# A rank-15 channel product over 512 tokens at once, with token-row products on GpSimd, in an RWKV-6 and MLP-mixer kernel

## The chip, the core and the metric

The kernel runs on one core of a Trainium2 chip. The metric is the time of one execution in device microseconds; a comparison uses the median of several runs. The engines are TensorE (PE in the profile, its weight loads PEld), VectorE (DVE), ScalarE (ACT), GpSimd (POOL) and SyncE (SP). Each works off its own queue in order.

## The reference

```python
B, H, S, D = 4, 8, 768, 48        # batches, heads, tokens, head size; H * D = 384
for t in range(S):                # RWKV-6: a state of D x D per batch and head
    y[:, :, t] = r_t @ (state + (u * k_t) v_t^T)
    state = w_t[:, :, :, None] * state + k_t v_t^T
x = y, laid as (B, S, 384)
u = x + (relu(x^T @ w_tok1) @ w_tok2)^T           # token mixing, 768 -> 256 -> 768
out = u + relu(u @ w_ch1) @ w_ch2                 # channel mixing, 384 -> 1536 -> 384
```

All in float32.

## The kernel before

**Units.** The recurrence is cut into 12 units of 256 tokens, three to a batch. A unit runs two scans on VectorE over the decays w (`ends` with the reciprocal, L368 to L373, and `begins`, L380), multiplies keys and queries by their results (`keys` L377, `queries` L383), turns the keys on TensorE (`tokens`, L287, tile k_ps), forms outer products (`carry`, L303), carries the state (`updates` on VectorE, `scaled` on ScalarE, L438), and forms gram matrices (L257) and the outputs y_ps (`before` L317, `after` L338). `products` (L400, L402, L405) are three VectorE instructions per unit on the tile `near`: r times k, times u, summed over a head. In the last eight units they stand for the term of a token with itself; the tile is loaded by SP (`load_near`).

**Mixing.** Per batch: `hidden` and `back` are the token mixing (L522, L529), `turn` transposes its result into xT (L537). The first channel product is plain in the first batch (`up`, 256 tokens wide, L547). In the other batches it is `thirds`: 15 products (L585) of 4 matmuls each in place of a 3 by 3 by 2 block product's 18, for 256 tokens in two blocks of 128. `rights` makes the sums of its right sides on VectorE (L572, L499). Each product goes to a PSUM bank named x, y, z, u, v, w or q, several of which collect more than one; from there ScalarE copies (`take`, L590) or VectorE adds or subtracts (`plus` L593, `minus` L596, `rest` L599) into z, and ScalarE applies the relu (`done`, L602). A bank is written again only when the tap before has read it.

The second channel product is plain (`down`, 24 matmuls 384 wide, L624) for the first two of the first batch's three stretches of 256 tokens, and `quarters` otherwise: seven products p1 to p7 of six matmuls 192 wide (L642, L646) in place of a 2 by 2 block product's eight, with four sums of z on VectorE (L689, L690), three of them into tiles of their own, and with u2 and u3 summed on VectorE.

**Order.** It is written by hand: each batch is a list of pieces, and `woven` merges lists so that each is spread evenly by its pieces' costs; the merged order is the order of every engine's queue. The mixing of one batch is woven with the units of the next. In the first batch the sums of the weights (`weight_sums` L486, `left_sums` L503 to L508) are woven into the second channel product. PSUM has six banks for all of this (`ps_m`) and two for `carry`.

The order of the second and third batch is written in

```python
pieces = woven(hiddens + turned[:6] + sums[:3] + ..., a0 + a1 + a2 + b0)
for s, (att, near) in enumerate(((b1, n + 1), (b2 + c0, n + 2), (c1 + c2, n + 3))):
    ...
    pieces += ups[:1] + woven(ups[1:11], products_of(near) + sums[:2]) + ups[11:] + woven(att, ...quarters(s)...)
```

where a, b and c are the next batch's three units, each in three parts (0: loads and `ends`; 1: `keys` to `carry`; 2: `gram` to the end).

Of the kernel before, what the change touches and what calls it, by code (L numbers as in the profile page):

```python
# [62 lines left out]
def rwkv6_then_mixer(  # L63
# [48 lines left out]

    rks = [const.tile([128, 2 * COLS], f32, name=f"rk{i}") for i in range(3)]
# [37 lines left out]
    def load_near(i):  # L151
        if UB < i < NU:
            nears[i] = apool.tile([128, UC, 2, DM], f32, name="near", bufs=1)
            sp.dma_start(nears[i], near[i - UB - 1])
# [34 lines left out]
    early = [t.bitcast(u32) for t in halves]  # L189
    bits64 = [t[:, :4 * PIECE] for t in (scratch, spare, early[0])]  # L190
# [155 lines left out]
    def unit(i):  # L346
# [50 lines left out]
        def products(n):  # L397
            t = nears[i]
            if n == 0:
                dve.tensor_mul(t[:, :, 0], t[:, :, 0], t[:, :, 1])  # L400
            elif n == 1:
                dve.tensor_mul(t[:, :, 0], t[:, :, 0], u_rows.unsqueeze(1).to_broadcast([128, UC, DM]))  # L402
            else:
                L["sums"] = apool.tile([128, UC, H], f32, name="sums")
                dve.tensor_reduce(out=L["sums"], in_=nears.pop(i)[:, :, 0].rearrange("p c (h e) -> p c h e", e=D),  # L405
                                  axis=mybir.AxisListType.X, op=ALU.add)
# [58 lines left out]
        def each(f, n):  # L465
# [4 lines left out]
                    own_put=own_put, products=[lambda n=n: products(n) for n in range(3)], sums_put=sums_put,  # L470
# [4 lines left out]
    z_sums = [halves[0][:, ts(i, HJ * 128)].rearrange("p (j t) -> p j t", j=HJ) for i in range(3)]  # L475
    w_sums = [scratch[:, ts(i, HJ * HM)].bitcast(f32).rearrange("p (j e) -> p j e", j=HJ) for i in range(3)]
    parts = halves[0][:, ds(3 * HJ * 128, 3 * HM)].rearrange("p (n e) -> p n e", n=3)
    late_sums = [t.rearrange("p q x t -> p (q x t)")[:, :HJ * 128].rearrange("p (j t) -> p j t", j=HJ) for t in ats]
    late_sums.append(starts[:, :HJ * 128].rearrange("p (j t) -> p j t", j=HJ))
    late_parts = ws[0][:, :3 * HM].rearrange("p (n e) -> p n e", n=3)  # L480
# [32 lines left out]
    def mixing(bt, x_of, out_rows):  # L513
# [5 lines left out]
        def hidden(i, c):  # L519
            if c == 0:  # L520
                sums[i] = ps_m.tile([128, DM], f32, name="h1_ps", tag="m")
            pe.matmul(sums[i], wtok1[:, c, ts(i, 128)], x_of()[:, c, :], start=(c == 0), stop=(c == C - 1))  # L522
            if c == C - 1:
                act.activation(h1[:, i, :], sums.pop(i), AF.Relu)  # L524
# [15 lines left out]
        def up(s, jt, blocks=range(DM // 128)):  # L540
            if jt == 0 and 0 in blocks:
                zs[s] = halves[int((bt, s) != (0, 0))].rearrange("p (j t) -> p j t", j=NJ)
# [9 lines left out]
        def rights(s):  # L552
            b = lambda k, m: xT[:, k, ds(s * SEG + m * 128, 128)]
            if not last:
                four = h1.rearrange("p i e -> p (i e)")[:, :512] if s % 2 else rights_at[:, 8 * 128:]
                eight = rights_at[:, :8 * 128]
            elif s % 2 == 0:
                near = apool.tile([128, 12 * 128], f32, name="near", bufs=1)
                four, eight = near[:, :512], near[:, 512:]
            else:  # L560
                eight, four = apool.tile([128, 8 * 128], f32, name="to_end"), apool.tile([128, 4 * 128], f32, name="kT", bufs=1)
            h, f, e, g = (four[:, ts(n, 128)] for n in range(4))
            r12, r13, r9, r0, r4, r7, r2, r10 = (eight[:, ts(n, 128)] for n in range(8))
            of = {0: r0, 1: b(0, 1), 2: r2, 3: b(0, 0), 4: r4, 5: f, 6: b(2, 1), 7: r7, 8: b(1, 0), 9: r9, 10: r10, 11: e,
                  12: r12, 13: r13, 14: g}
            hfe = four[:, :3 * 128].rearrange("p (k t) -> p k t", k=3)
            first, second = (xT[:, :, ds(s * SEG + m * 128, 128)] for m in range(2))
            sums = ((dve.tensor_add, g, b(0, 1), b(1, 1)), (dve.tensor_add, hfe, first, second), (dve.tensor_sub, r12, b(0, 0), e),
                    (dve.tensor_sub, r13, b(0, 0), b(2, 0)), (dve.tensor_add, r9, r13, g), (dve.tensor_sub, r0, b(2, 1), b(1, 0)),
                    (dve.tensor_add, r4, f, h), (dve.tensor_sub, r7, h, e), (less, r2, b(1, 1), b(2, 1)),  # L570
                    (dve.tensor_add, r10, b(1, 0), b(2, 0)))
            return of, [(0.05, lambda q=q: q[0](*q[1:])) for q in sums]  # L572

        def thirds(s, of):
            z = halves[s % 2 if last else 1].rearrange("p (j t) -> p j t", j=NJ)
            to = lambda n: z[:, ts(n // 2, JB), ts(n % 2, 128)]
            banks = {}

            def product(r, name, end):
                first = name not in banks  # L580
                if first:
                    banks[name] = bank("z_ps").rearrange("p (q t) -> p q t", q=JB)
                ps = banks[name]
                for q in range(JB):
                    pe.matmul(ps[:, q], lefts[r][:, ts(q, 128)], of[r], start=first and q == 0, stop=end and q == JB - 1,  # L585
                              skip_group_check=True)
                return ps

            def take(n, ps):
                act.copy(to(n), ps)  # L590

            def plus(n, ps):
                dve.tensor_add(to(n), to(n), ps)  # L593

            def minus(n, ps):
                dve.tensor_sub(to(n), to(n), ps)  # L596

            def rest(n, ps):
                dve.tensor_sub(to(n), ps, to(n))  # L599

            def done(n, ps):
                act.activation(to(n), to(n), AF.Relu)  # L602

            order = ((14, "x", False, [(take, 3)]), (8, "y", False, [(take, 2)]), (12, "z", False, [(take, 4)]),
                     (9, "x", False, [(plus, 2)]), (0, "y", False, [(minus, 4)]), (4, "u", False, [(take, 0)]),
                     (13, "x", True, [(minus, 0), (take, 1)]), (5, "y", False, [(take, 5)]), (6, "v", False, [(plus, 5)]),
                     (7, "z", True, [(plus, 1)]), (2, "y", True, [(plus, 3), (done, 3)]), (10, "u", True, [(rest, 2), (done, 2)]),
                     (3, "w", True, [(minus, 0), (minus, 4), (done, 0)]), (1, "q", True, [(plus, 5), (plus, 1), (done, 5), (done, 1)]),
                     (11, "v", True, [(minus, 4), (done, 4)]))

            def one(r, name, end, taps):
                ps = product(r, name, end)
                for f, n in taps:
                    f(n, ps)

            return [(0.9, lambda q=q: one(*q)) for q in order]

        def down(s, n, jts):

            if jts[0] == 0:  # L620
                sums[n] = ps_m.tile([128, DM], f32, name="h2_ps", tag="m")
# [9 lines left out]
        def quarters(s):  # L631
            z = halves[s % 2 if last else 1].rearrange("p (j t) -> p j t", j=NJ)
            a11, a12, a21, a22 = (z[:, ts(j, HJ), ts(i, 128)] for i in range(2) for j in range(2))
            s1, s2, s4 = late_sums if last else z_sums
            t1, t2, t4 = w_sums
            m1, u2, u3 = ((late_parts if last else parts)[:, i] for i in range(3))
            L = {}

            def begin(a, b):
                L["q"] = ps_m.tile([128, HM], f32, name="q_ps", tag="m")  # L640
                for j in range(HJ // 2):
                    pe.matmul(L["q"], a[:, j, :], b[:, j, :], start=(j == 0), stop=False)  # L642

            def product(a, b):
                for j in range(HJ // 2, HJ):
                    pe.matmul(L["q"], a[:, j, :], b[:, j, :], start=False, stop=(j == HJ - 1))  # L646
                return L.pop("q")
# [4 lines left out]
            def p1():  # L652
                o = L["o"] = mpool.tile([128, 2, DM], f32, name="o", bufs=1)
                x = L["x"] = x_of()[:, ts(s, 2), :]
                act.copy(m1, product(a11, w11))
                dve.tensor_add(o[:, 0, :HM], x[:, 0, :HM], m1)

            def p4():
                o, x = L["o"], L["x"]
                dve.tensor_add(o[:, 1, :HM], x[:, 1, :HM], product(a22, t4))  # L660

            def p2():
                o = L["o"]
                dve.tensor_add(o[:, 0, :HM], o[:, 0, :HM], product(a12, w21))

            def p5():
                o, x = L["o"], L["x"]
                dve.tensor_add(o[:, :, HM:], x[:, :, HM:], product(s1, t1).unsqueeze(1).to_broadcast([128, 2, HM]))

            def p6():  # L670
                o = L["o"]
                dve.tensor_add(u2, m1, product(s2, t2))
                dve.tensor_add(o[:, 0, HM:], o[:, 0, HM:], u2)

            def p7():
                o = L["o"]
                both = o[:, 1].rearrange("p (n e) -> p n e", n=2)
                dve.tensor_add(u3, u2, product(a21, w12))
# [283 lines left out]
```

## Time and profile before

| | us |
|---|---|
| median of 3 runs (lowest, highest) | 517.13 (515.79, 517.88) |
| the profiled execution | 515.98 |
| its span | 514.3 |
| PE busy in the span | 489.3 (95%) |
| DVE busy | 388.3 (76%) |
| ACT busy | 229.3 (45%) |
| POOL busy | 1.3 |

The profile is of one execution; its span is from the first to the last instruction on the core, and the execution's own time is 1.7 us longer. A row of a group or of the timeline names the line of the kernel, the engine, the operation, the tile written and the tiles read. Each float32 matmul of the program has two rows. "Idle before" is the time in which an engine had nothing to run just before a row, with the instruction that ended it.

### The profile page before, as it was taken

The page shows a single profiled execution, that of the slowest core. Times are in us where ns is not written, and L with a number is a line of the kernel's source. Part 1 is how long each engine was busy: PE and PEld are TensorE (multiplying, and loading weights), DVE is VectorE, ACT ScalarE, POOL GpSimd, SP SyncE. Part 2 cuts the span into 40 slices and gives each one's busy share as a digit, 9 for nine tenths or more (in the row PEclk, how much of TensorE's full clock was granted, in tenths as well). Part 3 has the DMA queues.
Part 4 walks back from the last instruction along what each step waited for, and adds up shares of the span by engine and source line. Part 5 has one row for each costly group of instructions (what it writes and reads, how often), then busy time and mean ns, then how long its engine had stood idle before and what let it go on. Part 6 is the DMA issues. An engine that isn't in the chain of part 4 may idle for free.

```text
span 514.3 us, 13327 instructions
## 1 busy us (share of the span) xinstructions
PE 489.3 (95%) x5794; PEld 427.6 (83%) x5794; DVE 388.3 (76%) x633; ACT 229.3 (45%) x533; POOL 1.3 (0%) x10
## 2 busy tenths in 40 slices
PE   3489999999999999999999999999999999999996
PEld 2476688766789768999999868999999859999996
DVE  7999979959886878967888768977758616684653
ACT  3977685635353535434335445434335413531300
POOL 0000000000000000000000000000000000000000
PEclk9789999999999999999999999999999999999998
DMA  7945965352532342122212422100000000000000
GB/s 294 322 178 159 270 209 175 116 178 62 163 108 91 97 135 64 62 73 78 78 44 79 138 74 64 63 32 1 2 32 1 28 5 1 1 2 34 1 33 34
DMA packets 20945, 46.06 MB, mean 90 GB/s; under 512 B 2128, under 2 KB 13008, under 8 KB 20880
## 3 DMA queue, kind: packets, MB, share of 16 engines
q1 hardware_dynamic: 20736, 45.14, 27.4%
q8 instruction: 47, 0.77, 0.6%
q14 instruction: 18, 0.15, 0.1%
q10 hardware_dynamic: 144, 0.00, 0.0%
HBM read 40.41 MB, written 4.72 MB: 88 GB/s over the span
## 4 chain that ended last, share of the span: by engine, by line
PE 81%; DVE 12%; ACT 3%; issue 2%; DMA 1%; SPq 0%; DVEq 0%; ACTq 0%
PE z_ps L585 18%; PE q_ps L646 12%; PE q_ps L642 11%; PE z_ps L547 9%; PE h_ps L624 6%; PE h_ps L529 6%; PE h_ps L522 6%; PE gram L257 2%; PE y_ps L317 2%; PE y_ps L338 2%; PE kv_ps L303 2%; PE xT_ps L537 2%; DVE z L593 2%; DVE w L380 2%; ACT z L602 1%
## 5 line engine op out<-in xcount | busy, mean ns | idle before, releaser
L438 ACT ACTIVATE before<-state,to_end 112x48 f32<-112x48 f32 x176 | 44.5, 324 | 66.4 <-DVE state L448 61.0
L590 ACT COPY z<-z_ps 128x512 f32<-128x512 f32 x54 | 30.5, 586 | 57.5 <-PE z_ps L585 39.5
L593 DVE TENSOR_TENSOR z<-z,z_ps 128x512 f32<-128x512 f32 x54 | 35.9, 683 | 24.5 <-PE z_ps L585 15.9
L602 ACT ACTIVATE z<-z 128x512 f32<-128x512 f32 x54 | 33.3, 631 | 33.1 <-DVE z L593 29.0
L547 PE MATMUL z_ps<-xT,wch 128*128 128x256 f32 x216 | 48.1, 381 | 0.0
L547 PEld LDWEIGHTS z_ps<-xT,wch 128*128 128x128 f32 x216 | 40.5, 190 | 5.7
L646 PE MATMUL q_ps<-wch,z 128*128 128x192 f32 x222 | 43.3, 331 | 0.0
L642 PE MATMUL q_ps<-wch,z 128*128 128x192 f32 x222 | 42.8, 329 | 0.2
L642 PEld LDWEIGHTS q_ps<-wch,z 128*128 128x128 f32 x222 | 36.5, 190 | 0.9 <-ACT z L602 0.6
L646 PEld LDWEIGHTS q_ps<-wch,z 128*128 128x128 f32 x222 | 36.5, 190 | 0.6
L529 PE MATMUL h_ps<-h,wtok 128*128 128x384 f32 x96 | 34.9, 492 | 0.6 <-ACT h L524 0.6
L596 DVE TENSOR_TENSOR z<-z,z_ps 128x512 f32<-128x512 f32 x45 | 30.0, 683 | 7.0 <-PE z_ps L585 6.5
L522 PE MATMUL h_ps<-x,wtok 128*128 128x384 f32 x96 | 33.1, 492 | 0.0
L624 PE MATMUL h_ps<-wch,z 128*128 128x384 f32 x96 | 33.1, 493 | 0.0
L531 DVE TENSOR_TENSOR x<-x,h_ps 128x384 f32<-128x384 f32 x24 | 13.2, 551 | 24.5 <-PE h_ps L529 24.5
L585 PE MATMUL z_ps<-rk,wch 128*128 128x128 f32 x256 | 31.2, 275 | 0.0
L585 PEld LDWEIGHTS z_ps<-rk,wch 128*128 128x128 f32 x256 | 30.0, 192 | 0.0
L372 DVE TENSOR_TENSOR_SCAN to_end<-w,starts 112x1041 f32<-112x1041 f32 (+1 forms) x13 | 28.1, 2160 | 2.1 <-DMA w<-in_w_dram 1.7
L380 DVE TENSOR_TENSOR_SCAN w<-w,starts 112x1041 f32<-112x1041 f32 x12 | 27.8, 2321 | 0.0
L646 PE MATMUL q_ps<-scratch,z 128*128 128x192 f32 x144 | 27.8, 329 | 0.0
L642 PE MATMUL q_ps<-scratch,z 128*128 128x192 f32 x144 | 27.4, 327 | 0.0
L585 PE MATMUL z_ps<-xT,wch 128*128 128x128 f32 x216 | 27.1, 275 | 0.0
(183 smaller groups left out, 903.1 us busy)
## 6 DMA issues: line engine op xcount, KB each, us to landing
rk<-in_rk_dram SPq DMA_DIRECT2D x36, 192.0 KB, 3.9
near<-in_near_dram SPq DMA_DIRECT2D x8, 768.0 KB, 4.3
w<-in_w_dram SPq DMA_DIRECT2D x11, 520.5 KB, 3.8
vt<-in_v_dram SPq DMA_DIRECT2D x12, 384.0 KB, 3.4
out_dram<-o SPq DMA_DIRECT2D x24, 192.0 KB, 1.9
spare<-in_w_ch_dram SPq DMA_DIRECT2D x8, 512.0 KB, 4.8
scratch<-in_w_ch_dram SPq DMA_DIRECT2D x8, 512.0 KB, 4.8
rk<-in_rk_dram SPq DMA_DIRECT2D x6, 512.0 KB, 8.7
```

The source lines that it names most:

```text
L380: dve.tensor_tensor_scan(w_[:ROWS], w_[:ROWS], starts[:ROWS], 0.0, op0=ALU.mult, op1=ALU.add)
L438: act.mul(t[:ROWS, a], state[bt, g][:ROWS, a], by_last(c, j)[:, a:a + 1])
L522: pe.matmul(sums[i], wtok1[:, c, ts(i, 128)], x_of()[:, c, :], start=(c == 0), stop=(c == C - 1))
L529: pe.matmul(ps, wtok2[:, i, ts(c, 128)], h1[:, i, :], start=(i == 0), stop=(i == DTOK // 128 - 1))
L547: pe.matmul(ps, wch1[:, m, ts(jt, 128)], xT[:, m, ts(s, SEG)], start=(m == 0), stop=(m == DM // 128 - 1))
L585: pe.matmul(ps[:, q], lefts[r][:, ts(q, 128)], of[r], start=first and q == 0, stop=end and q == JB - 1, skip_group_check=True)
L590: act.copy(to(n), ps)
L593: dve.tensor_add(to(n), to(n), ps)
L602: act.activation(to(n), to(n), AF.Relu)
L624: pe.matmul(ps, zs[s][:, jt, ts(n, 128)], wch2[:, jt, :], start=(jt == 0), stop=(jt == NJ - 1))
L642: pe.matmul(L["q"], a[:, j, :], b[:, j, :], start=(j == 0), stop=False)
L646: pe.matmul(L["q"], a[:, j, :], b[:, j, :], start=False, stop=(j == HJ - 1))
```

## The change

The rank-15 product covers the first 512 tokens of a batch at once, in blocks of 256: `rights(0)` makes sums 256 wide, and `thirds(0)` goes through its left side in two halves (`at` 0 and 2), so that a bank still holds 128 x 512. The last 256 tokens keep blocks of 128. Some sums are made in place in xT.

`quarters` makes its sums in place in z; p1, p6 and p7 go one after the other into one PSUM bank (`chain`), from a pool of one (`ps_h`), and `ps_m` has five banks. The pool of one also takes bank z of `thirds`, one bank of `hidden` and one of `down`. The first batch's second stretch of 256 tokens gets `quarters` too, so that the sums of the weights move: sums 0 to 2 into the plain product, sum 3 and all ten left sums into the quarters after it.

In the second and third batch the two multiplications of `products` go to GpSimd, with the tile's load issued by ScalarE just before them; the sum over a head stays on VectorE, some ten products of the rank-15 product later. `ends` and `keys` of the second unit move from the front into the middle of the rank-15 product; the third unit's `ends` goes into the product of the last 256 tokens.

```diff
-        def products(n):
+        def products(n, by=dve):
...
-            b = lambda k, m: xT[:, k, ds(s * SEG + m * 128, 128)]
+            width = SEG if s == 0 else SEG // 2
+            b = lambda k, m: xT[:, k, ds(s * SEG + m * width, width)]
...
+            by_half = s == 0
+            count = JB // 2 if by_half else JB
...
-                for q in range(JB):
-                    pe.matmul(ps[:, q], lefts[r][:, ts(q, 128)], of[r], ...)
+                for q in range(count):
+                    pe.matmul(ps[:, q], lefts[r][:, ts(at + q, 128)], of[r], ...)
...
+            chain = (p1, p6, p7)
+
+            def begin(p, a, b):
+                if p in chain[1:]:
+                    L[p] = L[chain[0]]
+                else:
+                    L[p] = (held if p in chain else bank)("q_ps")[:, :HM]
+                half(0, L[p], a, b, first=p not in chain[1:])
...
+            of = {p1: (a11, w11), p4: (a22, t4), p2: (a12, w21), p5: (a22, t1), p6: (a11, t2), p7: (a21, w12), p3: (a12, w22)}
+            sum1 = (0.01, lambda: dve.tensor_add(a22, a21, a22))
+            two = [*ps[p1], *ps[p4], sum1] if start == 1 else [*ps[p4], sum1, *ps[p1]]
+            return [*two, (0.01, lambda: dve.tensor_sub(a21, a11, a21)),
+                    (0.01, lambda: dve.tensor_sub(a11, a22, a11)), *ps[p2], (0.01, lambda: dve.tensor_sub(a12, a12, a11)), *ps[p5], *ps[p6],
+                    *ps[p3], *ps[p7]]
...
-        downs = [plain(s) if bt == 0 and s < 2 else quarters(s) for s in range(S // SEG)]
+        downs = [plain(s) if (bt, s) == (0, 0) else quarters(s, 4 if (bt, s) == (0, 2) else 1) for s in range(S // SEG)]
...
     def products_of(i):
-        return [(1.0, f) for f in units[i]["products"]] + [(0.1, lambda: load_near(i + 1))] if i < NU else []
+        first, second, sums = units[i]["products"]
+        return [(0.1, lambda: load_near(i, act)), (0.1, lambda: first(by=pool)), (0.1, lambda: second(by=pool)), (1.0, sums)]
...
+        begin, scan, key, *b1 = *b0, *b1
+        loads, *c0 = c0
+        pieces = woven([e for h in hiddens for e in h] + turned[:5] + sums[:1] + turned[5:9], a0 + a1 + a2)
+        pieces += [begin, *sums[1:3], turned[9], *sums[3:]]
+        ups, first, second, third = with_turned(turned, thirds(0, of)), products_of(n + 1), products_of(n + 2), products_of(n + 3)
+        pieces += ups[:1] + first[:3] + ups[1:14] + first[3:] + ups[14:18] + [scan, key] + ups[18:20] + second[:3] + ups[20:31] + second[3:] + ups[31:]
+        of, sums = rights(2)
+        pieces += woven(b1, woven(quarters(0), sums))
+        ups = thirds(2, of)
+        pieces += ups[:1] + third[:3] + c0 + ups[1:14] + third[3:] + ups[14:]
+        pieces += woven(b2 + [loads] + c1 + c2, quarters(1) + quarters(2, 4))
...
-            mixed = downs[0][4:] + downs[1][:4] + woven(downs[1][4:] + ups[2], of_weights + [(0.1, f) for f in left_sums()])
+            left = [(0.1, f) for f in left_sums()]
+            mixed = woven(downs[0][4:], of_weights[:3]) + woven(downs[1], left[:3] + of_weights[3:] + left[3:]) + ups[2]
```

`with_turned` puts the last two `turn`s of a batch behind the first and second of the rank-15 product's pieces, and in the last batch the same `thirds(0)`, `quarters(0)`, `thirds(2)`, `quarters(1)`, `quarters(2, 4)` follow one another without units.

## The prediction

> **What bounds the kernel now.** I read the page first: busy times and the slices.
>
> ```profile
> PE 489.3 (95%) x5794; PEld 427.6 (83%) x5794; DVE 388.3 (76%) x633; ACT 229.3 (45%) x533; POOL 1.3 (0%) x10
> ...
> PE   3489999999999999999999999999999999999996
> ...
> DVE  7999979959886878967888768977758616684653
> ```
>
> TensorE (PE) is full from the fourth slice on; VectorE (DVE) comes second. Matmul ends are modelled, so I asked for the stages by window (us; busy PE, PEld, DVE, ACT, POOL; clock): the first batch's second channel product, the second batch, the fourth batch.
>
> ```profile
> 93.30:174.00 80.70, 80.09 (x1078) 61.02 (x1077) 64.02 (x90) 36.37 (x100) 0.00 (x0) 1.00 0.38 115
> 174.00:291.90 117.90, 117.61 (x1439) 107.08 (x1438) 94.98 (x161) 51.61 (x125) 0.00 (x0) 1.00 0.26 82
> ...
> 409.80:509.50 99.70, 99.40 (x680) 91.76 (x679) 55.21 (x114) 26.12 (x48) 0.00 (x0) 1.00 0.03 12
> ```
>
> PE idles 0.3 to 0.6 us in each, at full clock. What it waited for at all, from the view of waits for PE:
>
> ```profile
> PE gram L257 <- DMA rk<-in_rk_dram: 8.8, 1, 8.8
> PE y_ps L317 <- ACT before L438: 2.7, 2, 2.1
> ```
>
> The first is the start. So the end is set by PE's work, and a saved matmul pays in full as long as DVE, in its own strict order, stays ahead of PE. Matmul prices are in the chain of waits (start, us, what; two rows for one fp32 matmul of the program):
>
> ```profile
> 63.97 29.36 PE z_ps L547 x136
> ...
> 95.49 5.16 PE h_ps L624 x16
> ...
> 199.09 11.61 PE z_ps L585 x104
> ...
> 211.68 0.97 PE q_ps L646 x6
> ```
>
> Per program matmul: 256 wide 29.36/68 = 0.432, 384 wide 0.645, 128 wide 11.61/52 = 0.2233, 192 wide 0.324 us. The 128-wide one is dear: half of a 256-wide one is 0.216.
>
> DVE's prices come from the groups, its real pace from the timeline:
>
> ```profile
> L593 DVE TENSOR_TENSOR z<-z,z_ps 128x512 f32<-128x512 f32 x54 | 35.9, 683 | 24.5 <-PE z_ps L585 15.9 <-ACT z L590 8.1
> L690 DVE TENSOR_TENSOR z<-z 128x768 f32<-128x768 f32 x10 | 9.5, 951 | 0.0
> ```
> ```profile
> 118.28 0.07 DVE L368 MEMSET starts<- 112x17 f32 x1
> 118.39 2.33 DVE L372 TENSOR_TENSOR_SCAN to_end<-w,starts 112x1041 f32<-112x1041 f32 x1
> 120.74 0.26 DVE L373 RECIPROCAL starts<-to_end 112x16 f32<-112x16 f32 x1
> 120.92 1.29 DVE L486 TENSOR_TENSOR scratch<-wch,scratch 128x1152 f32<-128x1152 f32 x1
> 122.13 1.21 DVE L377 TENSOR_TENSOR rk<-rk,to_end 112x1024 f32<-112x1024 f32 x1
> 123.25 2.32 DVE L380 TENSOR_TENSOR_SCAN w<-w,starts 112x1041 f32<-112x1041 f32 x1
> ...
> 126.23 1.04 PE L287 MATMUL k_ps<-ident,rk 128*128 128x128 f32 x8
> ```
>
> Neighbours overlap by about 0.08 (the 1.21 row is followed 1.12 later), so I use paces: 0.60 for a 128x512 tap (an L593 row), 0.87 for a 128x768 sum, 0.27 for a 128x192 tap, 2.64 for memset, scan and reciprocal, 1.25 for L486. See also that this scan ran 8 us before PE needed its keys at 126.23: nothing in front of it waited for PE.
>
> **The change: PE's work.** First batch, second 256 tokens: 24 matmuls of 0.645 (15.48) become 42 of 0.324 (13.61): -1.87. Second to fourth batch: of 180 matmuls of 0.2233, 120 become 60 of 0.432: -26.80 + 25.91 = -0.89 each, -2.67. Together **-4.54 us**.
>
> **What lies beside PE.** Sums in place and one accumulating bank (`chain`) take two DVE taps and an ACT copy (L655) from each set of quarters; ACT is 45% busy and DVE has slack there: 0. Wider sums of the right side: product 8 needs none, the others become ready at the pace of 0.36 each and PE takes 0.86 per product: 0. Five shared banks and one held: the accumulators that PE reuses are freed in time by the taps, except as below; without that cover each late tap costs PE its delay.
>
> The ten token-row products go from DVE (0.95 each) to GpSimd. No row shows one there. Their load is now issued on ACT's queue just before them (SP's issue of it is a 0.34 row, 5 of them on ACT: hidden) and lands after 4.3 us (median of the DMA view); DVE reaches the sum that needs them some 11 us after the issue, so two may take 6.7 together. Lower end 0.95 each, upper end three times that, 2.85: both hidden, so 0; above 3.3 each, the sum blocks DVE. [...]
>
> What moves on other queues: the loads of unit n+1 (SP) stand behind the front instead of in it, some 15 us ahead of the keys that need them, and land in 3.9 us: 0. Of the weight sums 0 to 2, now in the plain product, 0 and 1 fall into DVE gaps (the tap at 112.29 had 4.97 of idle time before it): 0; sum 2 is (a).
>
> **Where DVE becomes late.** Laid out in queue order, with code names.
>
> (a) First batch, end of the plain product. Weight sum 2 (1.25) now stands in DVE's queue in front of the tap and the mask that in the trace started at 113.58 and 114.05. The tap moves to 114.28, the mask to 114.75, the state update ends at 116.33, ACT's four products (1.01) at 117.4. PE ends the plain product at 113.34, its first quarter at 115.28, and y_ps (1.27) would end at 116.55; its second half needs ACT: 117.5. **+0.95**. The same wait is in the trace:
>
> ```profile
> 168.57 0.99 PE L317 MATMUL y_ps<-before,rk 48*64 48x48 f32 x28 [0.61 <-ACT before L438]
> ```
>
> (b) First batch, quarters 1. DVE may only overwrite a22 when PE has ended p4. Queued behind that are, in this order: p4's tap 0.27, three sums 2.61, weight sum 3 1.25, p2's tap 0.27, memset, scan and reciprocal 2.64, a left sum 0.60, a sum 0.87, the keys 1.21: 9.7, with releases 9.9 us after p4. PE has after p4 `after` (1.28), p2, p5, p6 (1.94 each): 7.1, and then the transposes that need the keys. **+2.8**. Who waits: all of PE. Then left sum, p5's tap, left sum, scan (2.23), p6's tap: 4.1 more, to 14.0; p7 must not touch the held bank before; PE has done transposes and p3 (1.30 + 1.94) by 13.15: **+0.9**. The ten left sums, spread over 28 us before, are now in these 14.
>
> (c) Second and third batch. `ends` and `keys` (3.77) stand in DVE's queue after the first half of the rank-15 product. From the end of product 10, DVE has: its tap, the reduction 0.86, five taps, 3.77 and product 9's tap, 0.60 x 6 + 0.86 + 3.77 + 0.08 + 0.68 = 9.0, before product 13 may use bank x again; PE needs 9 products of 0.864 = 7.8 until then. **+1.3 each, +2.6**. The last relus do not add to it: the latest is needed only by p4's fifth matmul, 0.2 later. In the fourth batch there is no scan: 0.
>
> (d) The last tap is p7's (0.55) instead of p3's (0.35): +0.2.
>
> **Sum.** The profiled execution took 515.98 (span 514.3 and 1.7 around it), 1.15 below the median of 517.13: 515.98 - 4.54 + 0.95 + 2.8 + 0.9 + 2.6 + 0.2 = 518.9; on the median's scale **520.0**. About 0.5% (2.6 us) is what a measurement can tell from no change; the runs lie 2.1 us apart.
>
> **Rivals.**
> *No late DVE (faster).* Place: (b) and (c). If DVE's 9.7 us after p4 were below PE's 7.1, and its 9.0 below 7.8, the keys would be there and only the work would count: 511.6, on the median's scale 512.8. For it: the trace hides far more DVE work than this, with PE idling under 0.7 us in each stage. Against: there the scan waited for nothing. Decides at 7.1 us from p4's end to the end of the keys.
>
> *Half of it (same).* Releases at single matmuls, or ACT and DVE catching up, halve (a) to (c): 518.9 - 3.6 = 515.3, 516.4 on the median's scale.
>
> *GpSimd slows DVE (slower).* The second pair of products runs beside the late taps of the second half. [...] By rows alone: a pair takes 1.9 to 5.7 us; if DVE lost half of the middle, 1.9 us, the relus that p1 and p4 wait for, which have 0.3 in hand, would be 1.6 late in two batches: 523.2.
>
> *Not what it says.* If 256-wide matmuls of this product ran at twice 0.2233, 2.67 of the gain would go: 522.7. Against it: L547 has the same width and operands.
>
> **Numbers.** Forecast 0.50, of it 0.36 above 519.7; GpSimd or pace 0.14, slower; half 0.16, same; no late DVE 0.20, of it 0.19 faster. So slower 0.50, same 0.31, faster 0.19. Range 513.0 to 523.5: it reaches up to the slow rivals and down to the fast one, of which it leaves out about 0.13, and 0.06 above.
>
> **What would show it.** PE's rows: 840 rows of q_ps become 924; 128-wide L585 rows fall to a third at the old pace and the new ones pace 0.216 per row. Right: in the first batch k_ps waits 2 to 3 us for DVE's keys and the first q_ps of p7 about 1 for DVE; in the second and third batch one z_ps waits about 1.3 for a DVE tap; POOL shows 10 products, each below 3.3. Wrong: PE idling less than 1 us in those stages (then 512 to 513), or q_ps waiting for ACT relus at the seam of the products (then above 522).

## The result: 4.85 us slower, and the profile after

The changed kernel took 521.28 us (median of 6 runs, 520.85 to 523.46), the kernel before beside it 516.43 (6 runs, 515.79 to 517.88). The ratio is 1.0093, its 95% interval 1.0074 to 1.0112. The profiled execution took 521.49, its span 519.7.

From the page: busy times, the slices of PE, and the clock that PE was granted.

```profile
PE 488.8 (94%) x5470; PEld 421.6 (81%) x5470; DVE 378.5 (73%) x588; ACT 225.3 (43%) x523; POOL 19.4 (4%) x20
...
PE   3678999997999999999999999999999999999995
...
PEclk9799999999899999999999999999999999999998
```

PE's tenth slice, up to 130 us, has become a 7, and the clock's eleventh, behind it, an 8. In the windows of the first batch's second channel product, the second batch, and the fourth batch with the end (us; busy PE, PEld, DVE, ACT, POOL; clock):

```profile
93.80:178.60 84.80, 80.56 (x1114) 67.41 (x1113) 68.91 (x99) 36.42 (x99) 0.00 (x0) 0.98 0.36 111
178.60:296.90 118.30, 116.53 (x1319) 102.03 (x1319) 88.37 (x142) 50.42 (x121) 10.89 (x6) 1.00 0.24 75
...
415.70:515.10 99.40, 98.79 (x560) 87.75 (x560) 52.79 (x99) 24.47 (x44) 0.00 (x0) 1.00 0.04 13
```

PE idles 4.24 us in the first, where it idled 0.61 before, and 1.77 in the second, where it idled 0.29. The view of waits for PE names the work it waits for (us in total, times, the longest):

```profile
PE k_ps L294 <- DVE rk L384: 2.9, 1, 2.9
PE y_ps L324 <- ACT before L445: 2.4, 2, 1.8
PE z_ps L606 <- DVE z L594: 2.3, 2, 1.1
...
PE h_ps L524 <- DVE starts L375: 1.3, 2, 0.6
...
PE h_ps L524 <- DVE o L672: 0.6, 1, 0.6
```

Three of these are the late keys, the late tap and (the shorter of the two of y_ps) the late weight sum of the prediction. The h_ps rows are a wait that the prediction did not have.

By stage, from the first matmul of one to that of the next in the two timelines (us; the spans are given to a tenth):

| stage | before | after | change | predicted |
|---|---|---|---|---|
| up to the plain product | 93.17 | 93.83 | +0.66 | 0 |
| first batch from there | 80.63 | 84.76 | +4.13 | +2.78 |
| second batch | 117.91 | 118.28 | +0.37 | +0.41 |
| third batch | 117.91 | 118.84 | +0.93 | +0.41 |
| fourth batch and end | 104.7 | 104.0 | -0.7 | -0.69 |
| span | 514.3 | 519.7 | +5.4 | +2.9 |

The first line has the same order of instructions in both kernels; over the fourteen traces of this case the plain product starts between 92.88 and 95.16. The experiments are therefore compared from there to the end of the span: 421.1 before, 425.9 after, +4.8.

**(a) and (b) in the timeline** (start, us, engine, what; in brackets the idle time before and what ended it), two answers, VectorE's rows and PE's:

```profile
123.71 1.35 DVE L488 TENSOR_TENSOR wch<-wch 128x1152 f32<-128x1152 f32 x1
...
125.40 2.33 DVE L379 TENSOR_TENSOR_SCAN to_end<-w,starts 112x1041 f32<-112x1041 f32 x1
...
129.34 1.22 DVE L384 TENSOR_TENSOR rk<-rk,to_end 112x1024 f32<-112x1024 f32 x1
...
134.38 0.33 DVE L664 TENSOR_TENSOR o<-o,q_ps 128x192 f32<-128x192 f32 x1
```
```profile
117.40 1.00 PE L324 MATMUL y_ps<-before,rk 48*64 48x48 f32 x28 [0.65 <-ACT before L445]
...
130.61 1.73 PE L294 MATMUL k_ps<-ident,rk 128*128 128x128 f32 x8 [2.94 <-DVE rk L384]
132.13 4.17 PE L639 MATMUL q_ps<-wch,z 128*128 128x192 f32 x18
...
242.46 3.19 PE L639 MATMUL q_ps<-wch,z 128*128 128x192 f32 x18
```

The queue is the one laid out, weight sum, scan, keys, and PE stands for 2.94 us until the keys are made. But look at what follows: the eight transposes take 1.73, while the other such groups between 94 and 300 us take 1.04, and 18 rows of q_ps take 4.17 instead of the 3.19 of such a group in the second batch (the last row). The windows there give the granted clock as the third number from the end:

```profile
131.00:132.00 1.00, 1.00 (x7) 1.00 (x6) 1.00 (x3) 0.48 (x1) 0.00 (x0) 0.50 0.00 0
...
134.00:135.00 1.00, 1.00 (x6) 1.00 (x6) 1.00 (x3) 0.00 (x0) 0.00 (x0) 0.84 0.00 0
```

In windows of half a us the half clock lasts from 130.91 to 134.32.

**(c) and the missing wait.** The middle of the second batch's rank-15 product, and the step from the first to the second batch:

```profile
217.20 2.33 DVE L379 TENSOR_TENSOR_SCAN to_end<-w,starts 112x1041 f32<-112x1041 f32 x1
...
219.74 1.16 DVE L384 TENSOR_TENSOR rk<-rk,to_end 112x1024 f32<-112x1024 f32 x1
220.81 0.67 DVE L594 TENSOR_TENSOR z<-z,z_ps 128x512 f32<-128x512 f32 x1
```
```profile
221.54 1.99 PE L606 MATMUL z_ps<-rk,wch 128*128 128x256 f32 x8 [1.13 <-DVE z L594]
```
```profile
177.98 0.56 DVE L672 TENSOR_TENSOR o<-o,q_ps 128x384 f32<-128x384 f32 x1 [2.27 <-PE q_ps L639]
```
```profile
178.59 1.88 PE L524 MATMUL h_ps<-x,wtok 128*128 128x384 f32 x5 [0.65 <-DVE starts L375]
```

The tap of product 9 comes behind scan and keys, and product 13 waits 1.13, in both batches. The last row is the new one: `hidden(0)` of the second to fourth batch puts its sum into the held bank, which p7 has just filled; PE can't begin the batch before p7's tap (L672) is done. That is 0.65 us three times. (The releaser in brackets, L375, is only the next instruction on VectorE.)

GpSimd's rows, and VectorE's tap, from the groups:

```profile
L407 POOL TENSOR_TENSOR near<-near 128x768 f32<-128x768 f32 x5 | 9.1, 1815 | 324.7 <-DMA near<-in_near_dram 313.1 <-DVE z L596 11.5
L594 DVE TENSOR_TENSOR z<-z,z_ps 128x512 f32<-128x512 f32 x54 | 35.7, 684 | 20.8 <-ACT z L590 11.8 <-PE z_ps L606 8.6
```

A product takes 1.81 us there, between the two bounds and hidden, and the tap beside it 684 ns as against 683 before.

### The profile page after: what moved, and what is told of

The parts are those of the page before. It is cut to its first block, busy times and chain, and to the rows that moved or that the text cites. A ratio compares the mean times of both kernels' runs of the same rounds, so it can differ in the third digit from the quotient of the medians.

```text
span 519.7 us, 12663 instructions
## 1 busy us (share of the span) xinstructions
PE 488.8 (94%) x5470; PEld 421.6 (81%) x5470; DVE 378.5 (73%) x588; ACT 225.3 (43%) x523; POOL 19.4 (4%) x20
## 4 chain that ended last, share of the span: by engine, by line
PE 85%; DVE 8%; DMA 4%; issue 2%; SPq 1%; ACT 0%; DVEq 0%
PE q_ps L639 29%; PE z_ps L606 20%; PE z_ps L549 9%; PE h_ps L531 6%; PE h_ps L524 6%; PE h_ps L625 3%; PE gram L264 2%; PE y_ps L324 2%; DMA w<-in_w_dram 2%; PE kv_ps L310 2%; PE y_ps L345 2%; DVE to_end L379 2%; DMA rk<-in_rk_dram 2%; PE k_ps L294 2%; PE xT_ps L539 2%
## 5 line engine op out<-in xcount | busy, mean ns | idle before, releaser
L639 PE MATMUL q_ps<-wch,z 128*128 128x192 f32 x528 | 96.1, 332 | 0.0
L639 PEld LDWEIGHTS q_ps<-wch,z 128*128 128x128 f32 x528 | 87.0, 192 | 1.5
L639 PE MATMUL q_ps<-scratch,z 128*128 128x192 f32 x396 | 69.0, 328 | 0.0
L639 PEld LDWEIGHTS q_ps<-scratch,z 128*128 128x128 f32 x396 | 64.5, 190 | 0.5
L549 PEld LDWEIGHTS z_ps<-xT,wch 128*128 128x128 f32 x216 | 40.6, 190 | 5.5
L606 PE MATMUL z_ps<-xT,wch 128*128 128x256 f32 (+1 forms) x240 | 42.6, 328 | 0.0
L606 PEld LDWEIGHTS z_ps<-xT,wch 128*128 128x128 f32 x240 | 36.4, 191 | 3.8 <-ACT z L590 0.8
L524 PEld LDWEIGHTS h_ps<-x,wtok 128*128 128x128 f32 x96 | 17.4, 190 | 13.2 <-DVE starts L375 1.9
L351 ACT COPY x<-y_ps 64x384 f32<-64x384 f32 (+1 forms) x36 | 17.1, 474 | 17.2 <-PE y_ps L345 16.8
L531 PEld LDWEIGHTS h_ps<-h,wtok 128*128 128x128 f32 x96 | 16.7, 190 | 9.4 <-ACT h L526 1.7
L647 DVE TENSOR_TENSOR o<-x,q_ps 128x192 f32<-128x192 f32 x22 | 7.8, 352 | 19.9 <-PE q_ps L639 15.6
```

The source lines that it names most:

```text
L531: pe.matmul(ps, wtok2[:, i, ts(c, 128)], h1[:, i, :], start=(i == 0), stop=(i == DTOK // 128 - 1))
L549: pe.matmul(ps, wch1[:, m, ts(jt, 128)], xT[:, m, ts(s, SEG)], start=(m == 0), stop=(m == DM // 128 - 1))
L606: pe.matmul(ps[:, q], lefts[r][:, ts(at + q, 128)], of[r], start=first and q == 0, stop=end and q == count - 1, skip_group_check=True)
L639: pe.matmul(ps, a[:, j, :], b[:, j, :], start=first and j == 0, stop=last and j == HJ - 1, skip_group_check=True)
```

## The experiments

The theory (W): PE's work did shrink, but PE now waits for VectorE, in the places of (a) to (c), at the held bank, and at half clock behind the longest wait. The rivals: VectorE is the bound as a whole, so that a wait taken away comes back at the next place (B); GpSimd's products disturb VectorE (P, G); the wide matmuls or the quarters do not save what their rows say. All runs were timed beside the kernel before; "from the start" means from the plain product's first matmul to the end of the span.

**e1, the held bank.**

```diff
-                sums[i] = (held if bt and i == 0 else bank)("h1_ps")[:, :DM]
+                sums[i] = (held if bt and i == 1 else bank)("h1_ps")[:, :DM]
```

> Against the changed kernel (span 519.7), one choice is altered: in the second to fourth batch the sum that uses the held bank is the second of `hidden` (i == 1), not the first (i == 0). The order of instructions is the same on every engine. Theory W (the time went into waits of PE for VectorE that the sum did not hold or sized too small): the first matmul of each batch no longer waits 0.65 us for p7's last tap; three rows of 0.65 go, the second `hidden` starts 1.95 us later when the tap has ended: -1.95 us, span 517.7, ratio to the kernel before about 1.0055. Rival B (VectorE as a whole is the bound, so that a wait taken away comes back at the next place): less than 0.7 us of it is seen, span above 519, and later waits grow by the rest. Rival P (GpSimd's reads disturb VectorE and PE): no change in the rows beside GpSimd; it says nothing on this run.

Measured: ratio 1.0054 (1.0037 to 1.0071); from the start 518.9 - 94.86 = 424.0, so -1.9. The three waits of h_ps are gone. In the second batch the transposes then wait 0.54 for keys that the 0.65 had covered; the third batch's stretch is 0.8 shorter. The missing term is shown.

```profile
183.38 1.09 PE L294 MATMUL k_ps<-ident,rk 128*128 128x128 f32 x8 [0.54 <-DVE rk L384]
```

**e2, the plain product back in the first batch.**

```diff
-        downs = [plain(s) if (bt, s) == (0, 0) else ...
+        downs = [plain(s) if bt == 0 and s < 2 else ...
...
-            mixed = woven(downs[0][4:], of_weights[:3]) + woven(downs[1], left[:3] + of_weights[3:] + left[3:]) + ups[2]
+            mixed = downs[0][4:] + downs[1][:4] + woven(downs[1][4:] + ups[2], of_weights + left)
```

> Against the changed kernel, one part is undone: the first batch's second 256 tokens get the plain product again (24 matmuls of 384 columns), and the sums of the weights and of the left side go back to where they were in the kernel before. Theory W: PE's work there grows by 1.87 us; the wait for weight sum 2 (0.65), the wait of the transposes for the keys (2.94) and the matmuls at a granted clock of 0.5 behind that wait (transposes 1.73 instead of 1.04, 18 rows of q_ps 4.17 instead of 3.19: 1.67) go: 1.87 - 5.26 = -3.4 us, span 516.3, ratio 1.002 to 1.003. The stretch from the plain product's start to the second batch falls from 84.6 to about 81.2. If only the waits counted and not the clock: -1.7. Rival S (the quarters save what they say, the loss is elsewhere): +1.9, span 521.6.

Measured: ratio 1.0030 (1.0018 to 1.0042); from the start 422.1, -3.8, and the first batch alone goes from 84.76 to 80.58, -4.18. Both waits and the half clock are gone (the transposes take 1.04 us again). The quarters, with the places of the sums that came with them, thus cost 4.18 net, while their rows promised to save 1.87.

**e3, only the left sums moved**, out of the quarters into the channel product behind them.

```diff
-            mixed = woven(downs[0][4:], of_weights[:3]) + woven(downs[1], left[:3] + of_weights[3:] + left[3:]) + ups[2]
+            mixed = woven(downs[0][4:], of_weights[:3]) + woven(downs[1], of_weights[3:]) + woven(ups[2], left)
```

> Against the changed kernel, only the place of the ten left sums changes: from the quarters of the first batch's second 256 tokens to the third stretch's first channel product behind them, where VectorE has little to do. Theory W: one left sum (0.6) no longer stands ahead of the keys, so the wait for them falls from 2.94 to about 2.3; what the clock does after a wait of 2.3 is not known: if it stays full, another 1.67 goes. So -0.6 to -2.3 us, and the squeezing of the left sums is the smaller part of (b); its larger part is the order scan, sums, keys behind p4. Rival B: the left sums pay later, in the third stretch, by as much: 0. Rival L (the left sums are the cause of the wait): the wait goes altogether, -2.9 to -4.6.

Measured: ratio 1.0072 (1.0056 to 1.0088); first batch 82.75, -2.01. PE's timeline and the windows behind the wait:

```profile
130.12 1.09 PE L294 MATMUL k_ps<-ident,rk 128*128 128x128 f32 x8 [2.44 <-DVE rk L384]
```
```profile
130.00:132.00 2.00, 1.88 (x14) 1.89 (x15) 2.00 (x3) 1.19 (x3) 0.00 (x0) 1.00 0.00 0
```

The wait fell by 0.50 only, but behind this wait of 2.44 the clock stayed full, and the other 1.5 us of the gain go with the clock. The left sums are thus the smaller part of (b). The 1.5 is not a clean price, though: the same edit also brought p6's tap forward, from 134.38 to 132.68, so that p7 had nothing else to wait for.

**e9, weight sum 3 late as well**, just ahead of p3, on top of e3.

```diff
-            mixed = woven(downs[0][4:], of_weights[:3]) + woven(downs[1], of_weights[3:]) + woven(ups[2], left)
+            mixed = woven(downs[0][4:], of_weights[:3]) + downs[1][:14] + of_weights[3:] + downs[1][14:] + woven(ups[2], left)
```

> Against the run with the left sums late: weight sum 3 (1.3 us), which only p7 needs, stands behind the keys and ahead of p3 in the first batch's quarters. Theory W: the wait of the transposes for the keys falls by 1.3, from 2.44 to about 1.15, the granted clock stays full, and p7 (its weight sum, then the held bank) does not wait: -1.3 us against that run, about -3.3 against the changed kernel, span about 516.4, ratio 1.0045. Even so the quarters would hardly pay there: they save 1.87 of PE's work and still wait 1.15 and 0.65. Rival L (p7 then waits for the late weight sum): 0 against that run.

Measured: ratio 1.0054 (1.0035 to 1.0073), first batch 82.77, no gain over e3. The wait for the keys fell to 1.18 as expected, but p7 then waited 1.16 for the weight sum, which had come to stand behind the scan and p6's tap: rival L, to the last tenth. In this stretch VectorE is behind by more than one instruction; it is not enough to move one.

**e4, the scan back in front** (second and third batch).

```diff
-        pieces = woven([e for h in hiddens for e in h] + turned[:5] + sums[:1] + turned[5:9], a0 + a1 + a2)
-        pieces += [begin, *sums[1:3], turned[9], *sums[3:]]
+        pieces = woven([e for h in hiddens for e in h] + turned[:5] + sums[:1] + turned[5:9], a0 + a1 + a2 + [begin, scan])
+        pieces += [*sums[1:3], turned[9], *sums[3:]]
...
-... + ups[14:18] + [scan, key] + ups[18:20] + ...
+... + ups[14:18] + [key] + ups[18:20] + ...
```

> Against the changed kernel, `ends` of the second unit (memset, scan and reciprocal, 2.64 us of VectorE) and the loads in front of it go back into the second and third batch's front, woven behind the first unit; `keys` (1.16) stays in the middle of the rank-15 product. Theory W: VectorE's queue before product 13 is 2.6 shorter, the wait of 1.13 goes in both batches: -2.26 us, span 517.4, ratio about 1.005; the front itself has room, as it had in the kernel before. Rival B: the scan comes to stand ahead of an addition that PE waits for in the front, 0.5 to 1.3 in each batch: 0 to -1.2. Rival P: the waits at product 13 stay at 1.1, since taps and products disturb each other: 0.

Measured: ratio 1.0147 (1.0126 to 1.0167), 2.3 us slower than the changed kernel from the start instead of 2.26 faster. Product 13 no longer waits, as W said, but the rank-15 product's sums (L572) now stand behind the scan: product 14, the second in order, waits 0.80 for them, and product 13 of the first half waits 1.28 for product 9's tap behind them. The timeline of that place has something else:

```profile
207.02 1.90 POOL L407 TENSOR_TENSOR near<-near 128x768 f32<-128x768 f32 x1 [205.06 <-PE z_ps L606]
207.18 2.03 DVE L572 TENSOR_TENSOR xT<-xT 128x256 f32<-128x256 f32 x1
```

A sum that takes 0.42 us elsewhere took 2.03, until GpSimd's product beside it had ended; the third batch has the same row at 326.89.

**e4b, GpSimd's first pair five products later**, on top of e4.

```diff
-        pieces += ups[:1] + first[:3] + ups[1:14] + first[3:] + ups[14:18] + [key] + ups[18:20] + ...
+        pieces += ups[:6] + first[:3] + ups[6:18] + first[3:] + [key] + ups[18:20] + ...
```

> The run with the scan in front, and GpSimd's first pair of products (with its load) five products later, the reduction behind it too. Theory G: the last sum of the rank-15 product's right side took 2.03 us there instead of 0.42 because GpSimd's product ran beside it; without that neighbour it takes 0.42, the wait of 1.28 behind it goes, and the wait of 0.80 for the sums stays: -2.6 us against that run, span about 519.3, ratio 1.009 to 1.010. Rival: the long row had another cause (a late operand): it stays at about 2, and nothing is gained.

Measured: ratio 1.0086 (1.0063 to 1.0110); from the start 425.2, 3.0 less than e4. The same row:

```profile
207.19 0.42 DVE L572 TENSOR_TENSOR xT<-xT 128x256 f32<-128x256 f32 x1
```

The wait of 1.28 is gone, that of 0.80 is left. So GpSimd did hold up this row, which reads two operands in SBUF. In the changed kernel no such row stands beside a product: there GpSimd's neighbours are taps, which read PSUM and took 0.69 there.

**e5, the products on VectorE again**, ahead of the reduction.

```diff
-        return [(0.1, lambda: load_near(i, act)), (0.1, lambda: first(by=pool)), (0.1, lambda: second(by=pool)), (1.0, sums)]
+        return [(0.1, lambda: load_near(i, act)), (0.1, lambda: None), (0.1, lambda: None), (1.0, lambda: (first(), second(), sums()))]
```

> Against the changed kernel, the ten token-row products go back to VectorE (0.95 us each, two together just ahead of the sum over a head that follows them); their loads stay where they are, so that PE's, ScalarE's and SyncE's orders are the same. Theory W: in the middle of the rank-15 product VectorE's queue gets 1.9 us more in front of product 13, and the wait of 1.13 grows to about 3.0 in the second and third batch; behind a wait of 2.9 the clock went to a half in the first batch, which cost about 1.5. So +3.7 without that and up to +6.7 with it, span 523.4 to 526.4, ratio 1.016 to 1.023. Rival P (GpSimd's products slow the rows of VectorE beside them, and that is where the time went): faster than the changed kernel, the waits of 1.13 shrink. Rival B (VectorE has slack for 1.9 us there): 0 to +1.

Measured: ratio 1.0305 (1.0277 to 1.0333), from the start 435.1, +9.2; slower still than W said. The waits at product 13 grew to 3.12 in both batches, and a wait of 1.70 for the last relus came up at the seam to the quarters of both. PE's rows behind the two long waits:

```profile
222.59 3.42 PE L606 MATMUL z_ps<-rk,wch 128*128 128x256 f32 x8 [3.12 <-DVE z L594]
```
```profile
346.69 1.99 PE L606 MATMUL z_ps<-rk,wch 128*128 128x256 f32 x8 [3.12 <-DVE z L594]
```

Behind the first the clock was at a half (0.50) until 225.5, behind the second, as long, it stayed full (1.00); the second batch grew by 5.3, the third by 4.0. The two batches had the same edit and the same waits, so the 1.3 between their growths is put down to that half clock. With this order of work the products belong on GpSimd.

**e8, only the keys behind the rank-15 product.**

```diff
-... + ups[14:18] + [scan, key] + ups[18:20] + ...
+... + ups[14:18] + [scan] + ups[18:20] + ...
...
-        pieces += woven(b1, woven(quarters(0), sums))
+        pieces += woven([key] + b1, woven(quarters(0), sums))
```

> Against the changed kernel, only `keys` (1.16 us of VectorE) of the second unit moves in the second and third batch: from the middle of the rank-15 product to the quarters behind it, where the kernel before had it; `ends` (2.64) stays in the middle. Theory W: VectorE has 2.6 instead of 3.8 in front of the tap that product 13 waits for, so the wait of 1.13 goes in both batches: -2.2 us, span 517.5, ratio 1.005. That half of the theory was seen with the scan put in front: product 13 waited no more, but the scan then stood ahead of the sums that the rank-15 product begins with (waits of 0.80 and 1.28 at its start). Rival B (what is taken away there comes back at the seam to the quarters, whose first tap now stands behind the keys): 0 to -1.

Measured: ratio 1.0090 (1.0070 to 1.0110); the two batches took 118.23 and 118.42 instead of 118.28 and 118.84, -0.5 in all. The waits of 1.13 are gone, but in both batches the quarters now wait 0.56 for VectorE's sums of z (L693), and one z_ps 0.24. Rival B was nearer: of 2.26 us of waits taken away, 0.5 stayed gained.

```profile
240.26 2.22 PE L639 MATMUL q_ps<-wch,z 128*128 128x192 f32 x12 [0.56 <-DVE z L693]
```

**e7, two matmuls of 128 columns for one of 256.**

```diff
-                    pe.matmul(ps[:, q], lefts[r][:, ts(at + q, 128)], of[r], ...)
+                    cols = [ts(n, 128) for n in range(2 if by_half else 1)]
+                    for n, c in enumerate(cols):
+                        pe.matmul(ps[:, q, c], lefts[r][:, ts(at + q, 128)], of[r][:, c], ...)
```

> Against the changed kernel, each matmul of 256 columns of the rank-15 product is issued as two of 128 (180 become 360); sums, taps and orders stay. Theory W by the rows of before: 2 x 0.2233 instead of 0.432 each, +0.0146 x 180 = +2.6 us, less what the longer products take from the waits of 1.13: +1.7 to +2.6, ratio 1.013 to 1.014. Rival (the width is worth nothing, 0.432 is two times 0.216 for any width): 0.

Measured: ratio 1.0132 (1.0111 to 1.0153), from the start 427.6, +1.7, while the waits of 1.13 shrank to 0.90. So the width is worth 1.7 + 0.5 = 2.2 us, against 2.63 by the rows: 0.74 in each batch instead of 0.89.

**e10, three repairs together**: e1, e2 and e8.

> Three repairs at once on the changed kernel: the held bank goes to the second sum of `hidden`, the first batch's second 256 tokens get the plain product, `keys` goes behind the rank-15 product. Theory W: -1.87, -4.17 and -2.2 add up, since they lie in different stretches: -8.2 us against the changed kernel. From the plain product's start to the end of the span that is 425.9 - 8.2 = 417.7, where the kernel before needs 421.1: faster than before by some 3.4 us, ratio 0.992 to 0.994. Rival B (VectorE is the bound as a whole): no faster than before, ratio 1.000 or above.

Measured: 514.44, ratio 0.9974 (0.9956 to 0.9991), from the start 419.3. Faster than before, by 1.8 instead of 3.4. The repair of e8 again brought far less than 2.2: the second and third batch took 117.73 and 117.62, where e1 without it took 118.14 and 118.04, 0.8 in all, and the quarters wait the same 0.56 in both.

**e11, the keys in a gap**: e10, with the keys four products behind the scan, and GpSimd's second pair four products later in the list (the expectation says six).

```diff
-... + ups[14:18] + [scan, key] + ups[18:20] + second[:3] + ups[20:31] + second[3:] + ups[31:]
+... + ups[14:18] + [scan] + ups[18:22] + [key] + ups[22:24] + second[:3] + ups[24:] + second[3:]
```

> The three-repairs kernel with one more change: in the second and third batch `keys` stands neither right behind `ends` nor at the seam to the quarters, but four products behind `ends`, and the second pair of GpSimd's products starts six products later than in the changed kernel. Theory W: VectorE has a gap there, so that the 0.56 which the first quarters waited for VectorE's sums in both batches goes, and no z_ps waits over 0.3: -1.1 us, about 418 from the plain product's start, ratio 0.995. Rival G (GpSimd's products hold up rows of VectorE that read two operands in SBUF; seen when the last of the rank-15 product's sums took 2.03 instead of 0.42 beside one): if the keys meet a product of GpSimd, their row grows from 1.2 to 2 or more and the gain is lost.

Measured: 515.40, ratio 0.9977 (0.9965 to 0.9989), from the start 420.0: no gain over e10. The keys' row is 1.22, so they met no product, but the reduction waited 0.57 for GpSimd, and the quarters 0.48 to 0.55 for the sums of z behind it.

**e12, all parts kept, the order repaired**: the changed kernel with e1, the order of e11, and in the first batch

```diff
-            mixed = woven(downs[0][4:], of_weights[:3]) + woven(downs[1], left[:3] + of_weights[3:] + left[3:]) + ups[2]
+            q, u = downs[1], ups[2]
+            mixed = woven(downs[0][4:9], of_weights[:3]) + downs[0][9:] + q[:7] + u[:5] + q[7:12] + of_weights[3:] + q[12:]
+            mixed += woven(u[5:], left)
```

> All parts of the change kept, and only the order repaired: held bank to the second sum of `hidden`; keys as in the run before; in the first batch the three weight sums earlier in the plain product, weight sum 3 ahead of p6 and p3, five parts of the third stretch's first channel product put between p4 and p2, and the ten left sums behind. Theory W: no k_ps wait over 1 us and full granted clock there, so the quarters pay what their work says: against the plain product of the run before, -1.87 of work, to which some 0.8 must be added for the starts of more and shorter groups (what was left over when the plain product was put back): first batch 78.7 instead of 79.8, ratio about 0.992. Rival B (VectorE is the bound in that stretch): PE waits as before somewhere else in it, first batch 80 or more, ratio 0.996 or above.

Measured: 514.17, ratio 0.9957 (0.9942 to 0.9972), from the start 418.9: 2.2 us less than before, 7.0 less than the changed kernel. The first batch takes 78.88 (78.7 was expected). All that PE still waits for behind 90 us:

```profile
PE q_ps L639 <- DVE z L690: 1.2, 2, 0.7
PE k_ps L294 <- DVE rk L384: 0.5, 1, 0.5
PE z_ps L606 <- ACT z L590: 0.4, 2, 0.2
PE y_ps L324 <- ACT before L445: 0.2, 1, 0.2
```

PE no longer waits over 0.3 us in the first batch. In e3 and e9, which moved sums but no matmul work, the keys still came 2.44 and 1.18 late, so the five pieces of matmul work between p4 and p2, which ask little of VectorE, are likely what gives it the time to make sums, scan and keys; no run moves them alone. The parts of the change do pay together; what made it slow was their order, and the place of the held bank.

## Why the prediction was right, and which of its steps were not

The sign and the reason held: PE's work shrinks by less than PE then waits for VectorE. The profiled execution was foretold at 518.9 and took 521.49; 0.66 of the difference lies in the start, the rest in these steps. That 521.28 lies only 1.3 from the 520.0 of the median's scale is partly luck: the kernel before came out at 516.43 beside it, 0.7 below the median that the forecast started from, so the change itself was foretold at 2.9 us and measured at 4.85, and the errors below have both signs.

- *PE's work, -4.54*: too large. 924 rows of q_ps and 0.2163 per row of the new L606 (chain: 40 rows in 8.65) are as foretold, but the two swaps brought less: the width 2.2 instead of 2.67 (e7); the quarters about 1.0 instead of 1.87 (e12 against e11: -0.89, with 0.20 of waits in it; e2: 4.18 is what is left of 0.65 + 2.94 + 1.5 less the work, so 0.9). The step multiplied a price out of the middle of long groups; the 42 short matmuls come in groups of 6 to 24 rows between attention's. That the starts of groups are what the rows leave out is argued from the row counts, not shown by a run.
- *(a)*: 0.65 instead of 0.95. Not in the sum: the wait of 0.61 of the kernel before at 168.57, shown under (a) as an example, is gone from the changed kernel, so that the two cancel.
- *(b)*: the wait for the keys was 2.94, 2.8 foretold. The second wait, 0.9 at p7, did not come. In its place PE lost 1.5 us to the half clock, which no step had. Worked out from the rows: at full clock p3 would have ended near 133.5 and p7 waited for p6's tap until 134.7; at half clock p3 ended near 135.2, past the tap. So at full clock the second wait would have come, some 1.2 us long, and by these rows the half clock took only 0.5 us beyond it.
- *(c)*: 1.13 twice instead of 1.3 twice (the prediction's own 9.0 and 7.8 are 1.2 apart); the rule that this lateness counts held, and e4 and e8 took it away in its place.
- *The step that failed* is the sentence on the six banks: "the accumulators that PE reuses are freed in time by the taps, except as below". I had followed the held bank to p7, but not past it, to the next batch's `hidden(0)`, which the diff puts there in a line of its own. 0.65 three times, 1.9 in the sum (e1).
- *(d)* and the fourth batch: -0.69 foretold, -0.7 measured. A match this close is chance: by e7 the width is worth less there too (104.8 against 104.0, so 0.8 instead of 0.89), and the same instructions took 104.4 in e2.
- *GpSimd*: 1.81 us a product, between the prediction's bounds of 0.95 and 2.85. The rival that GpSimd slows VectorE is wrong for the changed kernel (tap 684 and 683 ns) and right in kind: in e4 one row stood 1.6 us (2.03 instead of 0.42). That VectorE would lose half of the products' time was an estimate that no run shows.
- *No late VectorE* would have needed less than 7.1 us from p4 to the keys; it was 7.1 + 2.94. e12 comes near that rival's 512.8 with 514.17.

In the second batch the table has +0.37 and in the third +0.93, with the same waits. PE has the same 1318 rows in both and is busy 116.50 us in the one and 117.06 in the other. The 0.56 between them arises before the rank-15 product, where attention is woven in at other places; I did not follow it further.

## What to carry to other kernels

When PE is full and an edit saves matmul work, the time is decided by the queue of the engine that prepares PE's operands: lay that queue out from each buffer's release, and follow every bank to its next user, also past the end of the stage. A long wait can cost more than its length: here the clock stood at 0.50 for 3.41 us with each wait of 2.93 to 2.94 and with one of the two of 3.12, and stayed at 1.00 with those of 2.44 (e3) and 1.18 (e9); so a wait of 3 us is to be broken up before two of 1 us are. If a stage has too much VectorE work for its matmuls, weave in matmuls from a stage that has too little; moving single VectorE instructions within the stage mostly moved the wait (e4, e8, e9).

## What the runs showed of the hardware

**The clock.** After PE had idled 2.93 to 2.94 us, the granted clock fell to 0.50 in all seven kernels whose first batch had that wait, for 3.41 us each time by windows of half a us, beginning 0.3 to 1.2 us after PE had resumed; after 2.44 (e3) and 1.18 (e9) it stayed at 1.00, in one trace each; of the two waits of 3.12 in e5 it fell to 0.50 at one, from 222.11 to 225.52, which begins 0.48 before PE resumed, and stayed at 1.00 at the other. In e5 the batch with the fall grew by 1.3 us more than the one without; in e3 1.5 us went with it.

So the length of a wait alone does not decide in these traces: the two of 3.12 are equally long. What else does was not shown by a run.

**GpSimd beside VectorE.** In e4 a VectorE row with two operands in SBUF, begun 0.16 us after a GpSimd product, ended 0.29 us after that product's end and took 2.03 instead of 0.42. Taps with one operand in PSUM were not touched: in the changed kernel those begun inside a product took 0.69 (208.35, 252.06, 327.18, 341.61), the mean of all is 684 ns. No run changes the place of the operands alone, so that this is what makes the difference was not shown.
